# A fused retention, GLU and SwiGLU kernel: the last halved pair sends two sums at once, and the dealer that orders all instructions gets new costs, a second round and 137 shifts

## The chip, the cores and the metric

The kernel runs on one core of one Trainium2 chip. The metric is the device time of one execution in microseconds (us), the median of several runs. Before the change it is 615.1 us (three runs, 614.64 to 616.22).

## The reference, cut to what matters

```python
def reference(q, k, v, moe_w_a, moe_w_b, moe_w_out, moe2_w_gate, moe2_w_val, moe2_w_out, moe2_rms_g):
    # q, k, v: batch 2, 8 heads, 768 positions, head size 64
    for t in range(768):
        state = gamma * state + outer(k[t], v[t])        # per batch and head
        y[t] = q[t] @ state / sqrt(64)
    x = y as 1536 tokens x 512
    x = (x @ w_a) * (x @ w_b) @ w_out                    # feed-forward 0: 512 -> 1536 -> 512
    x = x / sqrt(mean(x * x) + 1e-6) * rms_g             # a norm over the 512 features
    g = x @ w_gate
    return (g * sigmoid(g)) * (x @ w_val) @ w_out        # feed-forward 1
```

## The kernel before, in words

The head of the program (about the first 97 us) computes the retention in chunks of 128 tokens: scores (tiles `sc`), their product with the values (`ya`), the running state (`st`). What follows are the two feed-forward blocks, 0 and 1. Features lie on the partitions, and the 1536 tokens are cut into three blocks j = 0, 1, 2 of 512. Each operand of a large product is split into a high and a low part in fp32r, so that one product of 128 x 128 weights with 512 tokens is three matmuls (high x high, high x low, low x high). In the tables of the trace these are the tiles `c`, `b` and `d` (going up, to 1536 features) and `y` and `x_P` (going down, back to 512).

**Halved products.** The 12 rows of 128 hidden features of a block are taken in pairs; a pair is numbered n = 6 * block + g. The first pair of a block is the opening one, the last the closing one, and the four between are "halved": for the token blocks 0 and 1 the down product is written as seven products of sums, P1 to P7, as in Strassen's scheme. Each exists twice (a and b, for two groups of 128 output features). P1 starts a bank of PSUM, which P6, P5 and P3 then add to (the tile is called `x4_P1_0` for half a of pair 4, whichever product adds to it); P7 starts a second bank, to which P4 adds (`x4_P7_0`); P2 has one to itself (`x4_P2_0`). After most of the products the bank as it then stands is one finished summand of the output. It is read by ScalarE (ACT) into one of four staging slots in SBUF (tiles `z`, in a ring), and sent from there by an accumulating DMA on GpSimd's queue (POOL) to `partial` (block 0) or `out` (block 1) in HBM. P5 has P7's bank added to its slot by VectorE (DVE) first. A halved pair makes 16 such sends, twelve from P products and four from the plain products `J` of token block 2.

```python
CHAIN = ("P1a P1b", "J", "J", "J", "J", "P7a P6a", "P5a P6b", "P4a P3a", "P7b P5b", "P3b P2a", "P4b P2b")
TO = {"P1": (0, 0, None), "P2": (0, 0, None), "P6": (1, 0, None), "P5": (1, 1, "Y2"), "P4": (1, 0, None), "P3": (0, 1, None)}
```

`CHAIN` is the order in which the products are recorded; an entry of `TO` says to which half of the output features and to which token block a sum goes, and which other bank is added. When a halved pair's sends have landed, the closing pair fetches the sums so far back from HBM by `fetch` (six loads of 512 KB into tiles `acc`, on SyncE's queue, SP), adds its own `y` products to them (`collect`, on DVE), and, in block 0, the norm follows: sums of squares over the partitions by matmul (`ms0`, `ms1`, `ms2`, one per token block), a short chain of small instructions on DVE and ACT that ends in `scale`, and a broadcast of it by matmul (`rb0`, `rb1`, `rb2`). `ms` and `rb` share one bank, which four multiplications on DVE read (`acc<-acc,small,rb`). In block 1 the sums are stored to `out`.

**What sets the order.** Nothing is issued as it is written. The kernel records every operation with the ones that it needs (`Plan.record`), an estimate of how long it occupies its engine and when its result is there. `Plan.order` works back from the end and gives each operation a due time. `Plan.list` (the dealer) then deals the operations out one by one: it follows each engine's time by the estimates, and of the operations that are ready takes the one that is due first. The resulting sequence is the program. So a change of an estimate, or a number added to one due time, moves instructions on all engines. Before, the dealer counted 100 ns for any change of the shape of the array's use on TensorE (PE), 100 + 0.83 n ns for any ACT instruction of n elements, and 60 ns from one engine to another.

All instructions of the kernel have one line in the profile, that of the call in `Plan.emit` (L435 before, L474 after); the tiles tell them apart.

Of the kernel before, what the change touches and what calls it, by code (L numbers as in the profile page):

```python
# [38 lines left out]
GRAIN = 4  # L39
AFTER = -1e6  # L40
AHEAD = 25
TURN = 100
TABLE = 1283
SHIFTS = {}
TABLES = AF.Silu, AF.Sqrt
LANES = 8
SOONEST = 12000
# [1 line left out]
DMA = {"load": (2400, 1.0, 600), "store": (700, 1.0, 600), "acc": (1750, 1.0, 600)}  # L49
RATE = {"load": 395, "store": 318, "acc": 145}  # L50
HOP = 120
LEAD = {"vec": 1850, "act": 1750, "gps": 4000}

LINE = 128
# [24 lines left out]
SOON = 400  # L79
GATE = "P5"  # L80
CHAIN = ("P1a P1b", "J", "J", "J", "J", "P7a P6a", "P5a P6b", "P4a P3a", "P7b P5b", "P3b P2a", "P4b P2b")
TO = {"P1": (0, 0, None), "P2": (0, 0, None), "P6": (1, 0, None), "P5": (1, 1, "Y2"), "P4": (1, 0, None), "P3": (0, 1, None)}
FORMS = "opening", *["halved"] * (NG - 2), "closing"
APART = 1
HOLD = {"vec": 1500, "act": 1200, "gps": 4000}
# [131 lines left out]
class Plan:  # L217
# [84 lines left out]
    def order(self):  # L302

        ops = self.ops
        for op in ops:
            for other in op.needs:
                other.next.append(op)
        hop = lambda a, b: (0 if a.engine == b.engine == "pe" and not a.kind else 28 if a.engine == b.engine and not a.kind else 85 if a.kind else 60) + (260 if b.engine == "gps" and b.kind else 0)
        took = lambda op, b: 0 if b.needs[op] == AFTER else DMA[op.kind][0] + DMA[op.kind][1] * op.length + DMA[op.kind][2] + b.needs[op] if op.kind else b.needs[op]
        nominal, t = {}, 0.0  # L310
        for op in ops:
            if op.engine == "pe":
                nominal[op] = t
                t += op.pitch
# [21 lines left out]
        return self.list({op: d + SHIFTS.get(op.name, 0) for op, d in due.items()}, hop)  # L336

    def list(self, due, hop):
        free, shape, table, port = dict.fromkeys(self.engines, 745.0), None, None, {"vec": 0.0, "gps": 0.0}
# [8 lines left out]
        lanes, arriving, queues, clock = {True: [], False: []}, [], {e: [] for e in ("sp", "act", "gps")}, 0.0  # L348

        def finish(op, end):  # L350
            for b in op.next:
# [9 lines left out]
        while len(done) < len(self.ops):  # L361
            best = None
            while at_pe < len(pe) and pe[at_pe] in done:
                at_pe += 1
            for e, some in able.items():
                if e == "pe":
                    last = pe[min(at_pe + AHEAD, len(pe)) - 1].index if at_pe < len(pe) else 0
                    some = [op for op in some if op.index <= last]
                if some:
                    at, lane = free[e], lanes[e == "gps"]  # L370
                    if e in ("sp", "gps") and len(lane) >= LANES and (e == "sp" or all(op.kind for op in some)):
                        if lane[-LANES] not in ended:
                            continue
                        at = max(at, ended[lane[-LANES]] + 85)
                    t = max(at, min(ready[op] for op in some))
                    if best is None or t < best[0]:
                        best = t, e, some
            moving = [q for q in queues.values() if q]
            total = sum(WEIGHT[q[0][1].kind] for q in moving)
            ends = [(clock + q[0][0] * total / WEIGHT[q[0][1].kind], n) for n, q in enumerate(moving)] + [(a[0], -1) for a in arriving]  # L380
            if ends and (best is None or min(ends)[0] <= best[0]):
                now, which = min(ends)
                for q in moving:
                    q[0][0] -= (now - clock) * WEIGHT[q[0][1].kind] / total
# [12 lines left out]
            op = min(now, key=lambda op: (due[op], op.index))  # L397
            if e == "pe":
                t += TURN * (shape not in (None, op.shape))
                shape = op.shape  # L400
            if op.table not in (None, table):
                t += TABLE
                table = op.table
            if op.port:
                t = max(t, port["vec" if e == "gps" else "gps"])
                port[e] = t + op.pitch
            able[e].remove(op)
            done.add(op)
            seq.append(op)
            start[op] = t  # L410
            free[e] = t + op.pitch
            if op.kind:
                arriving.append((t + DMA[op.kind][0], op.index, op))
                lanes[e == "gps"].append(op)
            for b in op.next:
                if b.needs[op] == AFTER:
                    ready[b] = max(ready[b], t)
                elif op.kind:
                    continue
                else:  # L420
                    ready[b] = max(ready[b], t + op.pitch if op.engine == b.engine == "pe" else t + b.needs[op] + hop(op, b))
                free_of(b)
        return max(free.values()), start, seq

# [14 lines left out]
def retention_glu_swiglu(ctx: ExitStack, tc: tile.TileContext, qk, kv, dq, mask, dg, eye, w1, w2, rg, partial, out):  # L439
# [5 lines left out]
    class Engine:  # L445
# [5 lines left out]
        def __getattr__(self, op):  # L451
            def issue(out, *a, **k):
                n = 1
                for size in out.shape[1:]:
                    n *= size
                at = work["pe"] + HOP if after_pe[0] is None else after_pe[0]
                pitch = self.fixed + n * self.each * (0.5 if op == "tensor_scalar" else 1)
# [3 lines left out]
                plan.record(self.name, op, out, a, k, pitch, pitch + 85)  # L461

            return issue

# [633 lines left out]
        collected.add(job)  # L1098
        tick()

    def pour(n, j, m, y, other=None):

        ffn, first = n // NG, FORMS[n % NG] == "opening"
        if (ffn, first) not in stages:
# [6 lines left out]
            act.copy(z, y)  # L1111
        else:
            vec.tensor_copy(z, y)
        if other is not None:
            add(z, z, other)
        to = (out if ffn else partial)[m, j]
        if first:
            dma("sp", to, z, ((ffn, m, j),))
        else:
            dma("gps", to, z, ((ffn, m, j),), accum_op=ALU.add)  # L1120

    def product_of_halves(n, name, i):

# [10 lines left out]
        y = chains[n, tag]  # L1134
# [31 lines left out]
    def do_down(k=1):  # L1166
        for _ in range(k):
# [6 lines left out]
            else:  # L1174
                for name in what.split():
                    product_of_halves(n, name[:2], "ab".index(name[2]))
                    if name == "P3b" and FORMS[g + 1] == "closing":
# [14 lines left out]
    def jobs(ffn, f, j):  # L1192
        n = ffn * NG + f // G
        if f % G == G - 1:
            if FORMS[n % NG] != "halved":
                todo.extend((n, (j, m)) for m in range(KD))
            elif j == 2:
                each = [(2, m) for m in range(KD)]
                todo.extend((n, each.pop(0) if what == "J" else what) for what in CHAIN)


    squaring, turns = [], [*PAIR, 2]
# [371 lines left out]
```

## Time and profile before

| | us |
|---|---|
| median of three runs | 615.1 |
| the profiled execution's own time | 616.86 |
| its span, from the first instruction to the last | 615.1 |
| PE busy | 601.9 |
| DVE busy | 525.4 |
| ACT busy | 418.2 |
| POOL busy | 124.8 |
| sends of 256 KB by accumulating DMA | 128 |

PE is TensorE's matmul unit, DVE VectorE, ACT ScalarE, POOL GpSimd, SP SyncE. Matmuls overlap in the records (one that is listed with 0.39 us starts 0.23 us after the one before), so a PE that is busy all the time is read by the distance of the starts, not by its share.

### The profile page before, as it was taken

How to read it: one execution, taken by the hardware profiler on the slowest of the kernel's cores; microseconds unless marked ns; L12 is line 12 of the kernel's file. 1: busy time of each engine (PE TensorE's matmuls, PEld its weight loads, DVE VectorE, ACT ScalarE, POOL GpSimd, SP SyncE). 2: the span in 40 equal slices, each digit the busy share in tenths (PEclk: the TensorE clock that was granted, in tenths of full speed). 3: DMA queues.
4: the chain of work that ended last, by engine and by line, in shares of the span. 5: the costliest groups of instructions: out<-in, count | busy, mean ns of one | idle time of the engine just before them, and what ended most of it. 6: DMA issues, size and time to landing. Idle time of an engine off the chain costs nothing.

```text
span 615.1 us, 9880 instructions
## 1 busy us (share of the span) xinstructions
PE 601.9 (98%) x3572; PEld 510.8 (83%) x3572; DVE 525.4 (85%) x949; ACT 418.2 (68%) x810; POOL 124.8 (20%) x142
## 2 busy tenths in 40 slices
PE   8999999999999999998999999999999999999997
PEld 8788888888888888886887778888888888888876
DVE  4789997799998997985788999699999899898554
ACT  3674786666886876685456867578888788787530
POOL 1330000013323323333100000001422323323310
PEclk9899999999999999998999999999999999999999
DMA  8984146039988988899950234424997997987895
GB/s 342 387 292 136 45 150 251 24 72 214 184 154 167 166 157 170 152 202 186 219 196 1 69 120 124 168 69 94 194 171 144 185 172 158 169 154 122 121 261 215
DMA packets 41617, 101.15 MB, mean 164 GB/s; under 512 B 4704, under 2 KB 5088, under 8 KB 41568
## 3 DMA queue, kind: packets, MB, share of 16 engines
q0 software_dynamic: 18432, 33.56, 37.8%
q1 hardware_dynamic: 22848, 66.79, 31.8%
q8 instruction: 28, 0.46, 0.3%
q14 instruction: 21, 0.17, 0.1%
q10 hardware_dynamic: 288, 0.17, 0.1%
HBM read 57.51 MB, written 42.99 MB: 163 GB/s over the span
## 4 chain that ended last, share of the span: by engine, by line
PE 86%; DMA 5%; DVE 5%; issue 1%; ACT 1%; DVEq 0%; SPq 0%; POOL 0%; ACTq 0%; POOLq 0%
PE b L435 29%; PE d L435 15%; PE y L435 15%; PE x_P L435 12%; PE c L435 9%; PE ya L435 3%; DVE acc L435 2%; DMA partial<-z 2%; PE sc L435 2%; DMA acc<-out 2%; DMA q<-in_qk 1%; PE w L435 1%; PE st L435 1%; ACT z L435 1%; DVE xl L435 1%
## 5 line engine op out<-in xcount | busy, mean ns | idle before, releaser
L435 POOL DMA_DIRECT2D out<-z x64 | 55.7, 910 | 230.5 <-ACT z L435 198.3
L435 POOL DMA_DIRECT2D partial<-z x64 | 55.9, 914 | 205.0 <-ACT z L435 172.5
L435 ACT COPY z<-x_P 128x512 f32<-128x512 f32 x96 | 55.4, 586 | 34.3 <-PE x_P L435 23.8
L435 PE MATMUL y<-h,o 128*128 128x512 f32 x288 | 68.7, 393 | 2.1 <-DVE acc L435 1.8
L435 PEld LDWEIGHTS y<-h,o 128*128 128x128 f32 x288 | 53.2, 188 | 14.2 <-DVE acc L435 2.7
L435 PE MATMUL b<-xh,uh 128*128 128x512 f32 x160 | 63.0, 394 | 0.0
L435 PE MATMUL b<-xl,uh 128*128 128x512 f32 x160 | 62.8, 392 | 0.0
L435 PE MATMUL b<-xh,ul 128*128 128x512 f32 x160 | 62.3, 389 | 0.0
L435 ACT CAST uh<-wt 128x512 fp32r<-128x512 f32 x82 | 48.9, 621 | 11.6 <-PE d L435 5.8
L435 DVE TENSOR_TENSOR ul<-wt,uh 128x512 fp32r<-128x512 f32 x82 | 53.0, 684 | 1.7 <-ACT uh L435 1.5
L435 PE MATMUL x_P<-r,l 128*128 128x512 f32 x192 | 51.8, 394 | 2.0 <-ACT z L435 2.0
L435 ACT ACTIVATE v<-raw 128x512 int32<-128x512 uint32 x72 | 48.7, 679 | 3.8 <-DMA raw<-in_w 3.4
L435 PE MATMUL y<-h,l 128*128 128x512 f32 x192 | 48.3, 391 | 0.0
L435 PE MATMUL b<-th,uh 128*128 128x512 f32 x120 | 47.7, 398 | 0.0
L435 PE MATMUL b<-tl,uh 128*128 128x512 f32 x120 | 47.6, 396 | 0.0
L435 PE MATMUL b<-th,ul 128*128 128x512 f32 x120 | 47.2, 393 | 0.0
L435 PE MATMUL d<-xh,ul 128*128 128x256 f32 x160 | 45.3, 283 | 0.0
L435 PE MATMUL d<-xl,uh 128*128 128x256 f32 x160 | 45.2, 283 | 0.0
L435 PE MATMUL d<-t,uh 128*128 128x256 f32 x240 | 45.0, 282 | 0.0
L435 PE MATMUL d<-xh,uh 128*128 128x256 f32 x160 | 45.0, 281 | 0.0
L435 PEld LDWEIGHTS d<-t,uh 128*128 128x128 f32 x240 | 40.4, 190 | 3.9
L435 DVE TENSOR_TENSOR g<-g,d 128x256 f32<-128x256 f32 x80 | 33.2, 416 | 11.1 <-PE d L435 5.2
(151 smaller groups left out, 1527.4 us busy)
## 6 DMA issues: line engine op xcount, KB each, us to landing
raw<-in_w SPq DMA_DIRECT2D x72, 512.0 KB, 5.1
partial<-z POOLq DMA_DIRECT2D x64, 256.0 KB, 5.2
out<-z POOLq DMA_DIRECT2D x64, 256.0 KB, 5.2
q<-in_qk SPq DMA_DIRECT2D x12, 512.0 KB, 5.6
k<-in_kv SPq DMA_DIRECT2D x12, 512.0 KB, 6.5
partial<-z SPq DMA_DIRECT2D x12, 256.0 KB, 2.5
acc<-partial SPq DMA_DIRECT2D x6, 512.0 KB, 5.8
out<-z SPq DMA_DIRECT2D x12, 256.0 KB, 2.8
```

The costliest lines, as they stand in the source:

```text
L435: getattr(self.engines[op.engine], method)(real(out), *map(real, args), **{k: real(a) for k, a in kwargs.items()})
```

## The change

The edits are three. First, the last halved pair of each block (pairs 4 and 10) is recorded in another order, and its sends are fewer. P2 is done beside P1 and its bank is added to P1's slot, so that the two go out as one send. P6's bank is copied to a slot that is kept; P4's bank is added to it later by DVE, and the sum goes out as one send. P2's banks are `Y2` and `B0` there. This makes eight fewer ACT copies, eight more DVE additions and eight fewer accumulating DMAs in the program (of 128); the matmuls are the same. The early part of the fetch of token block 1 is still tied to P3b.

Second, the dealer's estimates: the change of geometry on PE costs by kind (110 to 222 ns, 55 more in one case), an ACT instruction has one cost when it reads PSUM and one when it reads SBUF, and the distance between engines is 45 ns without POOL; idle time of PE that adds up is given a price of its own. The due times are computed twice, the second time from the order that the first deal gave. Third, 137 operations have their due time moved by -34 to +60 us.

```diff
-TURN = 100
+TURN = {(64, P): 200, (64, 64): 110, (P, P): 222, (P, 64): 147}
-SHIFTS = {}
+SHIFTS = {
+    4: -17300, 5: -11500, 6: -11100, 7: 3200, 8: -4300, 21: 17250, 36: 6800, 44: -4900, 45: 13450, 87: 21000, 89: 17100, 116: 32500, 117: -23300, 127:
...
+ROUNDS = 2
...
+ACT_COST = {False: (92, 0.836), True: (40, 0.855)}
...
-TO = {"P1": (0, 0, None), "P2": (0, 0, None), "P6": (1, 0, None), "P5": (1, 1, "Y2"), "P4": (1, 0, None), "P3": (0, 1, None)}
+TO = {"P1": (0, 0, None), "P2": (0, 0, None), "P6": (1, 0, None), "P5": (1, 1, "P7"), "P4": (1, 0, None), "P3": (0, 1, None)}
+WHEN = "P3b"
+CHAIN_LAST = ("P2a P1a", "P2b P1b", "J", "J", "J", "J", "P7a P6a", "P5a P6b", "P3a P4a", "P7b P5b", "P3b P4b")
+TO_LAST = {"P1": (0, 0, "P2"), "P6": "keep", "P5": (1, 1, "P7"), "P4": (1, 0, "kept"), "P3": (0, 1, None)}
...
+        pes = [op for op in ops if op.engine == "pe"]
+        for left in reversed(range(ROUNDS)):
+            due = self.dues(pes, took, hop)
+            got = self.list(due if left else {op: d + SHIFTS.get(op.index, 0) for op, d in due.items()}, hop)
+            pes = [op for op in got[2] if op.engine == "pe"]
+        return got
...
             if e == "pe":
-                t += TURN * (shape not in (None, op.shape))
+                if shape not in (None, op.shape):
+                    t += TURN[op.shape] + 55 * (shape == (64, 64) and op.shape == (P, 64))
...
-        tag = "Y2" if name in ("P7", "P4") else f"Y{i}"
+        last = FORMS[n % NG + 1] == "closing"
+        tag = ("Y2", "B0")[i] if last and name == "P2" else "Y2" if name in ("P7", "P4") else f"Y{i}"
...
-        if name in TO:
-            half, j, other = TO[name]
-            pour(n, j, 2 * half + i, y, chains[n, other.format(i)] if other else None)
+        to = (TO_LAST if last else TO).get(name)
+        if to == "keep":
+            chains[n, "kept", i] = stage(n, y)
+        elif to:
+            half, j, other = to
+            if other == "kept":
+                z = chains[n, "kept", i]
+                add(z, z, y)
+                send(n, j, 2 * half + i, z)
+            else:
+                pour(n, j, 2 * half + i, y, chains[n, other, i] if other else None)
```

Three places show how the dealt order moved. In all rows the number at the end of a name counts operations and differs between the two programs.

The first is ACT in the second half of pair 4, the last halved pair of block 0. Rows `z1_0` and `z1_1` fill the staging slots; `s9`, `t9`, `u9` free the bank `b1_9` of the up product beside it. Before:

```order
L435 COPY z1_0_1586<-x4_P1_1_2988 128x512
L435 COPY s9_3108<-b1_9_3090 128x512
L435 CAST h0_10_0_3114<-s8_2946 128x512
L435 COPY z1_0_1586<-x4_P7_0_3057 128x512
L435 CAST o10_3121<-wl10_3040 128x512
L435 COPY z1_1_1654<-x4_P1_0_2954 128x512
L435 COPY z1_1_1654<-x4_P1_1_2988 128x512
L435 COPY t9_3142<-b1_9_3090 128x512
L435 ACTIVATE wt12_3155<-raw12_0_3102 128x2x256
L435 COPY z1_0_1586<-x4_P1_1_2988 128x512
```

After the change, at the same place:

```order
L474 COPY s9_3101<-b1_9_3079 128x512
L474 CAST h0_10_1_3116<-u8_3077 128x512
L474 ACTIVATE v12_0_3124<-raw12_0_3088 128x512
L474 COPY z1_0_1534<-x4_P1_0_2901 128x512
L474 CAST o10_3139<-wl10_3055 128x512
L474 CAST h0_10_0_3142<-s8_2951 128x512
L474 COPY t9_3153<-b1_9_3079 128x512
L474 ACTIVATE wt12_3157<-raw12_0_3088 128x2x256
L474 COPY z1_1_1663<-x4_P1_1_2969 128x512
L474 COPY u9_3174<-b1_9_3079 128x512
L474 COPY z1_1_1663<-x4_P1_1_2969 128x512
```

Before, the copy of `x4_P7_0` (P4a) stands ahead of those of P3a and P5b. It is gone after the change: P4a's bank is read by DVE, which adds it to a slot that was filled at P6a. On PE, P7b, the next user of that bank, stood behind six matmuls after P4a before (P5b and P3a), and now stands behind 33: P3a, P5b and P3b of pair 4 and four blocks of six matmuls `b` lie between.

The second place is SP at the end of the program: the six loads of the sums so far for the closing pair of block 1, and the first store. The first number in `acc1_1_0` is the block, the second the token block j, the third the half of the output features. Before:

```order
L435 DMA acc1_1_1_6061<-out_0 128x2x512
L435 DMA acc1_2_1_6075<-out_0 128x2x512
L435 DMA acc1_2_0_6090<-out_0 128x2x512
L435 DMA acc1_1_0_6092<-out_0 128x2x512
L435 DMA acc1_0_0_6154<-out_0 128x2x512
L435 DMA acc1_0_1_6179<-out_0 128x2x512
L435 DMA out_0<-acc1_1_0_6092 128x512 x2
```

After:

```order
L474 DMA acc1_2_1_5962<-out_0 128x2x512
L474 DMA acc1_2_0_6080<-out_0 128x2x512
L474 DMA acc1_1_1_6083<-out_0 128x2x512
L474 DMA acc1_1_0_6108<-out_0 128x2x512
L474 DMA acc1_0_0_6137<-out_0 128x2x512
L474 DMA acc1_0_1_6148<-out_0 128x2x512
L474 DMA out_0<-acc1_1_0_6108 128x512 x2
```

The two loads of token block 2 moved to the front, ahead of the two of token block 1. On PE, the blocks between P3b of pair 10, whose send `acc1_1_0` waits for, and the first closing product `y68` were 33 matmuls of 512 columns and 36 of 256, and are 27 and 30 now; three closing products of six matmuls follow before `y71`, which needs the bank of `y68` again.

The third place is DVE in the norm, from the reciprocal of token block 2 to its `scale`. `o12` and `o13` are the out weights that `y40` and the products after it read. Before:

```order
L435 RECIPROCAL small_84<-small_84 128x4
L435 ISA u12_2_3593<-u12_2_3593,v12_2_3596 128x1024
L435 TENSOR_TENSOR small_84<-small_84 128x4
L435 ISA u13_2_3598<-u13_2_3598,v13_2_3608 128x1024
L435 SCALAR_TENSOR_TENSOR small_84<-small_84 128x4
L435 TENSOR_TENSOR g17_3633<-g17_3633,c17_1_3624 128x512
L435 SCALAR_TENSOR_TENSOR small_84<-small_84 128x4
L435 TENSOR_TENSOR acc0_1_1_3251<-acc0_1_1_3251,acc0_0_0_3365 128x1024
L435 CAST scale_3479<-small_84 128x4
L435 TENSOR_TENSOR g18_3685<-g18_3685,c18_1_3678 128x512
L435 TENSOR_TENSOR scale_3479<-small_84,scale_3479 128x4
```

After:

```order
L474 RECIPROCAL small_84<-small_84 128x4
L474 TENSOR_TENSOR o12_3624<-u12_2_3529,o12_3624 128x512
L474 TENSOR_TENSOR small_84<-small_84 128x4
L474 TENSOR_TENSOR h1_1_1_3644<-g16_3604,h1_1_1_3644 128x512
L474 SCALAR_TENSOR_TENSOR small_84<-small_84 128x4
L474 TENSOR_TENSOR o13_3646<-u13_2_3546,o13_3646 128x512
L474 SCALAR_TENSOR_TENSOR small_84<-small_84 128x4
L474 TENSOR_TENSOR acc0_1_0_3239<-acc0_1_1_3259,acc0_1_0_3239 128x1024
L474 CAST scale_3423<-small_84 128x4
L474 TENSOR_TENSOR g17_3668<-g17_3668,c17_1_3626 128x512
L474 TENSOR_TENSOR scale_3423<-small_84,scale_3423 128x4
```

The out weights' `o12` and `o13` now stand inside the chain, ahead of `scale`; before, they stood behind it. On PE, 36 matmuls of 512 columns lie between `ms2` and `rb2` now, and 30 before.

## Rows read from the trace of the kernel before

**Rows 1.** Page, part 1: busy us, share of the span, instructions.

```profile
PE 601.9 (98%) x3572; PEld 510.8 (83%) x3572; DVE 525.4 (85%) x949; ACT 418.2 (68%) x810; POOL 124.8 (20%) x142
```

**Rows 2.** Stages: us, busy us (instructions) per engine, PE clock, DMA share, GB/s.

```profile
100.00:283.00 183.00, 183.00 (x962) 157.34 (x961) 165.01 (x305) 128.00 (x244) 49.52 (x57) 1.00 0.80 159
...
306.00:358.00 52.00, 48.73 (x257) 40.15 (x256) 47.33 (x91) 35.10 (x55) 0.00 (x0) 1.00 0.27 87
358.00:597.00 239.00, 239.00 (x1246) 204.64 (x1245) 208.25 (x377) 177.47 (x342) 55.70 (x64) 1.00 0.74 153
...
286.40:289.80 3.40, 3.40 (x10) 2.63 (x9) 1.30 (x2) 1.06 (x3) 2.25 (x3) 0.50 0.80 100
```

**Rows 3.** Timeline of PE near 286 us: start, us, instruction, idle before.

```profile
285.83 1.18 PE L435 MATMUL x_P<-r,l 128*128 128x512 f32 x3 [1.97 <-ACT z L435]
286.80 0.63 PE L435 MATMUL b<-th,uh 128*128 128x512 f32 x1
287.23 0.63 PE L435 MATMUL b<-tl,uh 128*128 128x512 f32 x1
...
290.27 0.40 PE L435 MATMUL b<-xh,uh 128*128 128x512 f32 x1
290.50 0.40 PE L435 MATMUL b<-xl,uh 128*128 128x512 f32 x1
```

**Rows 4.** Chain of waits, 278 to 299 us: start, us, what.

```profile
278.52 6.57 DMA partial<-z
...
285.19 0.59 ACT z L435
...
285.83 1.18 PE x_P L435 x3
...
297.27 1.43 PE d L435 x12
```

**Rows 5.** Groups by line: busy us, mean ns, idle before.

```profile
L435 ACT COPY z<-x_P 128x512 f32<-128x512 f32 x96 | 55.4, 586 | 34.3 <-PE x_P L435 23.8 <-issue 5.6 <-DMA partial<-z 1.9
...
L435 DVE TENSOR_TENSOR z<-z,x_P 128x512 f32<-128x512 f32 x16 | 10.9, 681 | 1.6 <-ACT z L435 1.6
```

**Rows 6.** Page, part 6: DMA issues, KB each, median us to landing.

```profile
partial<-z POOLq DMA_DIRECT2D x64, 256.0 KB, 5.2
```

**Rows 7.** Timeline of PE in the closing of block 0 and the norm.

```profile
312.98 1.66 PE L435 MATMUL y<-h,o 128*128 128x512 f32 x6 [0.42 <-DVE acc L435]
...
329.99 1.02 PE L435 MATMUL ms<-small,sq 128*128 128x1 f32 x8 [0.74 <-DVE acc L435]
...
341.74 0.95 PE L435 MATMUL ms<-small,sq 128*128 128x1 f32 x8
...
350.90 0.30 PE L435 MATMUL rb<-ident,scale 128*128 128x128 f32 x1 [1.24 <-DVE scale L435]
351.47 1.00 PE L435 MATMUL rb<-ident,scale 128*128 128x128 f32 x7 [0.27 <-DVE scale L435]
...
353.93 3.24 PE L435 MATMUL y<-h,o 128*128 128x512 f32 x13 [0.26 <-DVE o L435]
```

**Rows 8.** Chain of waits, 575 us to the end.

```profile
580.90 1.36 PE x_P L435 x6
...
586.95 11.12 DMA acc<-out
```

**Rows 9.** Timeline of PE at the end.

```profile
598.90 12.58 PE L435 MATMUL y<-h,o 128*128 128x512 f32 x54 [1.34 <-DVE acc L435]
```

**Rows 10.** Timeline of DVE at the end.

```profile
611.52 0.76 DVE L435 TENSOR_TENSOR acc<-y,acc 128x256 f32<-128x256 f32 x2 [0.67 <-PE y L435]
```

**Rows 11.** DMA issues from 560 us on.

```profile
out<-acc SPq DMA_DIRECT2D x11, 256.0 KB, 2.1
```

**Rows 12.** Timeline of PE in the head.

```profile
24.96 0.50 PE L435 MATMUL c<-xh,uh 128*128 128x512 f32 x1
25.30 0.40 PE L435 MATMUL c<-xh,ul 128*128 128x512 f32 x1
```

More of the change, by code (lines that the diff above doesn't have):

```diff
@@ L41 @@
 AHEAD = 25
-TURN = 100
+TURN = {(64, P): 200, (64, 64): 110, (P, P): 222, (P, 64): 147}
 TABLE = 1283
-SHIFTS = {}
+SHIFTS = {
[12 rows of a table added]
+}
+ROUNDS = 2
+SLOW = 3414
+MOST = 2000
 TABLES = AF.Silu, AF.Sqrt
@@ L307, in order, with dues @@
                 other.next.append(op)
-        hop = lambda a, b: (0 if a.engine == b.engine == "pe" and not a.kind else 28 if a.engine == b.engine and not a.kind else 85 if a.kind else 60) + (260 if b.engine == "gps" and b.kind else 0)
+        hop = lambda a, b: (0 if a.engine == b.engine == "pe" and not a.kind else 28 if a.engine == b.engine and not a.kind else 85 if a.kind else 60 if "gps" in (a.engine, b.engine) else 45) + (235 if b.engine == "gps" and b.kind else 0)
         took = lambda op, b: 0 if b.needs[op] == AFTER else DMA[op.kind][0] + DMA[op.kind][1] * op.length + DMA[op.kind][2] + b.needs[op] if op.kind else b.needs[op]
+        pes = [op for op in ops if op.engine == "pe"]
[4 more added lines that the diff above has]
+        return got
+    def dues(self, pes, took, hop):
+        ops = self.ops
         nominal, t = {}, 0.0
[L311 to L314, printed above, removed]
+        for op in pes:
+            nominal[op] = t
+            t += op.pitch
         due, back = {}, {}
@@ L335, in order @@
                     heapq.heappush(heap, (-limit[a], -a.index))
-        return self.list({op: d + SHIFTS.get(op.name, 0) for op, d in due.items()}, hop)
+        return due
     def list(self, due, hop):
@@ L347, in list @@
         at_pe, done, start, ended, seq = 0, set(), {}, {}, []
-        lanes, arriving, queues, clock = {True: [], False: []}, [], {e: [] for e in ("sp", "act", "gps")}, 0.0
+        lanes, arriving, queues, clock, gaps, slow = {True: [], False: []}, [], {e: [] for e in ("sp", "act", "gps")}, 0.0, [], 0.0
         def finish(op, end):
@@ L406, in list @@
                 port[e] = t + op.pitch
+            pitch = op.pitch
+            if e == "pe" and t > 8000:
+                if t > free[e] + 1:
+                    gaps.append((free[e], t))
+                    while gaps[0][1] < t - SLOW:
+                        gaps.pop(0)
+                    if t >= slow and sum(b - max(a, t - SLOW) for a, b in gaps) > MOST:
+                        slow = t + SLOW
+                if t < slow:
+                    pitch = min(2 * pitch, pitch + slow - t)
             able[e].remove(op)
@@ L410, in list @@
             start[op] = t
-            free[e] = t + op.pitch
+            free[e] = t + pitch
             if op.kind:
@@ L420, in list @@
                 else:
-                    ready[b] = max(ready[b], t + op.pitch if op.engine == b.engine == "pe" else t + b.needs[op] + hop(op, b))
+                    ready[b] = max(ready[b], t + pitch if op.engine == b.engine == "pe" else t + b.needs[op] + pitch - op.pitch + hop(op, b))
                 free_of(b)
@@ L456, in issue @@
                 at = work["pe"] + HOP if after_pe[0] is None else after_pe[0]
-                pitch = self.fixed + n * self.each * (0.5 if op == "tensor_scalar" else 1)
+                ins = [v for v in (*a, *k.values()) if isinstance(v, View)]
+                banks = any(v.tile.pool.kinds for v in ins)
+                fixed, each = ACT_COST[banks] if self is act else (self.fixed, self.each)
+                pitch = fixed + n * each * (0.5 if op == "tensor_scalar" else 1)
+                pitch += 95 * (self is act and isinstance(k.get("scale"), View)) + 50 * (op == "scalar_tensor_tensor" and isinstance(a[1], View))
+                pitch += 45 * (self is act and any(v.dims[-1][0] > 1 for v in ins))
                 work[self.name] = max(work[self.name], at) + pitch
@@ L460, in issue @@
                 ends[0] = max(ends[0], last[0])
-                plan.record(self.name, op, out, a, k, pitch, pitch + 85)
+                plan.record(self.name, op, out, a, k, pitch, pitch + (105 if self is act else 85))
             return issue
@@ L1099, in down, with stage @@
         tick()
-    def pour(n, j, m, y, other=None):
+    def stage(n, y):
         ffn, first = n // NG, FORMS[n % NG] == "opening"
@@ L1113, in pour, with send @@
             vec.tensor_copy(z, y)
-        if other is not None:
-            add(z, z, other)
+        return z
+    def send(n, j, m, z):
+        ffn = n // NG
         to = (out if ffn else partial)[m, j]
-        if first:
+        if FORMS[n % NG] == "opening":
             dma("sp", to, z, ((ffn, m, j),))
@@ L1120, in pour @@
             dma("gps", to, z, ((ffn, m, j),), accum_op=ALU.add)
+    def pour(n, j, m, y, other=None):
+        z = stage(n, y)
+        if other is not None:
+            add(z, z, other)
+        send(n, j, m, z)
     def product_of_halves(n, name, i):
@@ L1176, in do_down @@
                     product_of_halves(n, name[:2], "ab".index(name[2]))
-                    if name == "P3b" and FORMS[g + 1] == "closing":
+                    if name == WHEN and FORMS[g + 1] == "closing":
                         after(FETCH, lambda: fetch(ffn, 1))
@@ L1198, in jobs @@
                 each = [(2, m) for m in range(KD)]
-                todo.extend((n, each.pop(0) if what == "J" else what) for what in CHAIN)
+                todo.extend((n, each.pop(0) if what == "J" else what) for what in (CHAIN_LAST if FORMS[n % NG + 1] == "closing" else CHAIN))
     squaring, turns = [], [*PAIR, 2]
```

2 lines of the change are left out of this document (1 added, 1 removed), and 11 rows, old and new, of the table SHIFTS.

## The prediction

> **What bounds the kernel now.** I read first how the span divides over the engines: PE is busy for 98% of it [rows 1]. Then the stages. From 100 to 283 us and from 358 to 597 us PE shows no idle time at all at the full clock [rows 2], and there the change, which leaves the matmuls as they are, has nothing to win. What it can win lies between these stages. The waits of PE over 0.2 us that I find behind the head stand in three places, and I went to each with the timeline and the chain of waits.
>
> The first is at 285.83 us: a product of pair 4 waits 1.97 us for an ACT copy into a staging slot [rows 3]. The chain shows why: that copy, 0.59 us long, waited for a send that took 6.57 us to land, because the slot that it fills was still being sent [rows 4]. So this stage is bound by the round of four slots, not by PE. Just behind the wait PE's clock falls to 0.50 of full speed, its lower level of 1.2 GHz, for 3.4 us [rows 2]: the matmuls of `b` start 0.43 us apart there and 0.23 us apart at 290.27 [rows 3]. For counting I use 0.227 us for a matmul of 512 columns and 0.119 us for one of 256, from runs of 6 and of 12 of them [rows 4, 8].
>
> The second place is the closing of block 0 and the norm. From 306 to 358 us PE is busy for 48.73 of 52.00 us [rows 2]; the larger waits are 0.42 us (a bank of `y` that DVE has yet to read), 0.74 us (`ms0`, behind the multiplications by `rb1`), 1.24 and 0.27 us (`rb2`, for the two parts of `scale`) and 0.26 us (the out weights) [rows 7]. The third is the end: `y71` waits 1.34 us [rows 9], because the load of the sums so far, issued at 586.95 us, took 11.12 us [rows 8].
>
> **The change part by part.** The sum is made on the profiled execution's span, 615.1 us, which is also the median of the runs; the 616.86 us of that execution itself are 1.8 us of surroundings that an unprofiled run doesn't show.
>
> *Pair 4's slots.* The product that waited is P7b, for P4a's bank. After the change no copy into a new slot frees that bank: DVE adds it to a slot that P6a filled long before. Between P4a and P7b there are 33 matmuls now, 33 x 0.227 = 7.5 us, and an addition like that takes 0.68 us [rows 5]. So the wait goes (-2.0) and with it, as I expect, the fall of the clock (3.4 x 0.5 = -1.7): -3.7. At worst both stay (0); more than -3.7 isn't there to win.
>
> The wait that could take its place: P5b's copy goes into the slot of P4a's sum, so it must wait for that send to land, and P3b on PE waits for the copy. From the end of P4a to P3b, PE has 30 matmuls, 30 x 0.227 = 6.8 us. The other side needs an addition (0.68), the landing (5.2 us in the median) and the copy (0.59) [rows 5, 6]: 6.5 us if nothing is queued ahead, 7.8 us with 6.57 us of landing as in the chain [rows 4]. That is a wait of 0 to 1.0 us; I take +0.4. A wait of 2.0 us with 1.7 of clock behind it would be the state before again. In pair 10 the same path has 9.0 us of cover (30 matmuls of 512 columns, 18 of 256), so nothing. The Trainium skill, in DMA: Bandwidth & Descriptors (section Anatomy of one DMA), gives a DMA from GpSimd as about 2.0 us and its bytes by 436 GB/s, which would be an estimated 2.6 us for these 256 KB. Half the median of the rows, so I go by the rows; by the page this term would be 0 and the time 0.4 us less.
>
> *The eight additions and copies.* 8 x 0.68 = 5.4 us more on DVE, 8 x 0.59 = 4.7 us less on ACT [rows 5]. They lie beside PE's work in stages where DVE is busy for 165.01 of 183 and 208.25 of 239 us [rows 2]; 2.7 us per block fit. If DVE had no room there, they would cost 2.7 us in each block. I cost them at nothing.
>
> *The norm.* `rb2` had 30 matmuls behind `ms2`, and its second part came 351.47 - 341.74 = 9.73 us after `ms2`, the first 9.16 us [rows 7]. Now there are 36, that is 6 x 0.227 = 1.4 us more, against 9.16 and 9.73 us that DVE's chain needs if it stays as long: it has the same small instructions, with seven large ones in between where there were eight. Of the 1.51 us some 0.5 stays: -1.0. The bank of `y` gets seven blocks instead of four until it is written again, and `o12` and `o13` now stand ahead of `scale`: -0.4 and -0.3. `ms0` has to wait for four multiplications that read the bank of `rb1`, with 2.8 us of `d` blocks as cover where there were 4.1 us of `y`; DVE has less between them. I leave its wait as it is. Together -1.7. From below, all 3.3 us go. From above, `ms0` and the product `c17_0` behind it lose 2 us: +2.0.
>
> *The end.* The loads of token block 2 are ahead of the two that matter, and four fewer sends are on their way beside them (two of them stood behind P3b). P3b ended at 580.90 + 0.68 = 581.58, the load was issued 5.4 us later [rows 8]. From P3b to `y71` there are 45 matmuls of 512 columns and 30 of 256 now, 45 x 0.227 + 30 x 0.119 = 13.8 us; before it was 51 and 36, 15.9 us, and the wait. So the load may take 13.8 - 5.4 = 8.4 us. With half of what it shared the DMA engines with gone, I estimate 6 to 7 of its 11.12 us: -1.3 for the wait (bounds 0 and -1.3). The last product is now one whose addition isn't cut in two: 0.68 us and then a store of 256 KB, 2.1 us in the median [rows 5, 11]. Before, both halves were added after 0.76 us [rows 10] and half the store was in flight by then: +0.2, bounds 0 and +0.7 (a third of that store).
>
> *Geometry.* The order of the program has 56 changes of geometry instead of 60, the four fewer all in the head. The first `c` after the state's matmuls is followed by the next after 0.34 us instead of 0.23 [rows 12], 0.11 us for a change: -0.4, between 0 and twice that. Up to the fourth chunk PE's order and the set of loads ahead of it are the same, so the start isn't faster.
>
> *Closer reuse of banks.* The new order is denser: a bank is written again behind only one block of other work in 41 places, where there were 15 (a `b` bank after 1.4 us 16 times against 9, a `d` bank after 0.7 us 6 times against 2, the rest among `x_P`, `b3` and `d3`). The 15 of before cost nothing, and a copy of 0.59 us [rows 5] fits into 1.4 us. But when another ACT instruction of 0.6 us is ahead of it in a place of 0.7 us, it doesn't. Between 0 and 26 x 0.6 = 15.6 us; the rows stand at nothing, I take +0.5.
>
> Sum: -3.7 + 0.4 - 1.7 - 1.3 + 0.2 - 0.4 + 0.5 = -6.0, so **609.1 us**.
>
> **The rivals.** (1) *The slots bind again.* The four slots are still a round, and a kept slot is held longer, from P6 to the landing of P4. If P5b's copy comes 2 us late, the clock falls as it did, and of the first term only the waits that moved are left: +3.3 on the forecast, 612.4 us. For it: sends were the bound of that stage. Against: the pair has 12 sends instead of 16. Chance 0.14. (2) *The norm empties.* All its waits go, the closer reuse costs nothing and the kept slot neither: -1.6 - 0.5 - 0.4, 606.6 us. For it: each of these waits is on a chain of small instructions that a few moved rows relieve. Chance 0.22. (3) *Slower: the closer reuse.* In the 26 added places PE waits for the reader of the bank, all over the two stages that had no wait. ACT is busy for 177.47 of 239 us there [rows 2], so an instruction is often ahead. From 0.3 us per place the sum turns: 26 x 0.3 = 7.8 us take the gain and more, 616.4 us, and 0.4 us give 619.0. Against: 15 such places show nothing. Chance 0.07 for over 616.9 us, 0.05 for between. (4) *The change of the sends works, the new deal does nothing*: the norm, the geometry and the banks stay as they are, and -3.7 + 0.4 - 1.3 + 0.2 = -4.4 is left, 610.7 us. For it: the estimates that changed differ by some tens of ns per instruction, and PE has no wait in most of the program. Against: the norm's rows did move. Chance 0.08.
>
> **How the numbers follow.** The forecast has a chance of 0.44, with 607.5 to 610.6 us for its own range; rival 2 has 0.22, rival 1 0.14, rival 4 0.08, rival 3 0.07 and 0.05. A difference of 0.3% (1.8 us) is about what a measurement can tell here. Slower is rival 3's 0.07; the same is its 0.05 and the upper edge of rival 1 (0.03); faster is the rest, 0.85. The range goes from 605.2 (rival 2 with the geometry at its bound, 606.2, and 1 us for stages that I counted as they are) to 613.3 us (rival 1 with the closer reuse at 1.4 instead of 0.5).
>
> **What would show it.** Right: no fall of the clock near 286 us, no wait of P7b; a load of `acc` near 580 us that lands in under 8.4 us and `y` products without a break to the end; a wait of about 0.5 us at `rb2`; 60 accumulating sends per block in place of 64. Wrong: PE idle behind P5b in pair 4 with ACT waiting for a landing; many waits of 0.2 to 0.6 us of PE for ACT between 100 and 283 or 358 and 597 us; a new wait at `c17_0`.

## The result and the profile after

The changed kernel takes 609.36 us in the median of six runs (606.94 to 611.52), the kernel before beside it 615.09; the ratio is 0.9905, 95% interval 0.9877 to 0.9932. That is 5.7 us less, where 6.0 were forecast. The places are not those of the forecast.

First the engines of the changed kernel (busy us, share, instructions), as in [rows 1]:

```profile
PE 598.6 (98%) x3572; PEld 509.6 (84%) x3572; DVE 528.8 (87%) x957; ACT 413.6 (68%) x802; POOL 117.1 (19%) x134
```

The eight additions and copies are there (957 for 949 on DVE, 802 for 810 on ACT, 8 fewer instructions on POOL). Next the stages, as in [rows 2]: us, busy us (instructions) of PE, PEld, DVE, ACT and POOL, PE's clock, DMA share, GB/s.

```profile
240.00:292.00 52.00, 49.04 (x232) 40.18 (x231) 40.40 (x71) 33.50 (x63) 15.91 (x20) 1.00 0.89 166
306.00:358.00 52.00, 50.95 (x257) 42.43 (x256) 50.20 (x94) 35.64 (x56) 0.00 (x0) 0.97 0.23 81
358.00:597.00 239.00, 239.00 (x1248) 205.27 (x1247) 208.56 (x382) 171.75 (x336) 52.15 (x60) 1.00 0.71 153
...
323.25:326.66 3.41, 3.41 (x9) 2.66 (x9) 3.23 (x8) 1.99 (x4) 0.00 (x0) 0.50 0.00 0
```

Two things are to be seen: PE is idle for 3 us around the last halved pair (240 to 292 us), and there is one stretch of the slower clock, now at 323 us, in the norm. Before, one lay at 286 us [rows 2] and another in the head, which is shown below. The waits themselves, in the timeline of PE (start, us, instruction, idle before):

```profile
250.55 0.96 PE L474 MATMUL x_P<-h,l 128*128 128x512 f32 x3 [1.14 <-ACT z L474]
...
273.81 0.97 PE L474 MATMUL x_P<-r,l 128*128 128x512 f32 x3 [1.68 <-ACT z L474]
...
321.68 1.02 PE L474 MATMUL ms<-small,sq 128*128 128x1 f32 x8 [0.76 <-DVE acc L474]
...
346.83 1.00 PE L474 MATMUL rb<-ident,scale 128*128 128x128 f32 x8
...
588.59 16.51 PE L474 MATMUL y<-h,o 128*128 128x512 f32 x72
```

The waits at `rb2` and at the end [rows 7, 9] are gone, and the 72 closing matmuls run without a break. P7b of pair 4 doesn't wait any more [rows 3]. In its place two other products wait for a copy into a slot: P3b of pair 3 (250.55) and P5a of pair 4 (273.81). They wait for the copies of P5b of pair 3 and of P6a of pair 4. The timeline of ACT says what those two copies waited for; the last line has the times from issue to landing of the sends of `z` between 238 and 276 us:

```profile
249.91 0.58 ACT L474 COPY z<-x_P 128x512 f32<-128x512 f32 x1 [1.02 <-DMA partial<-z]
...
273.17 0.58 ACT L474 COPY z<-x_P 128x512 f32<-128x512 f32 x1 [2.15 <-DMA partial<-z]
...
DMA to landing us min/median/max: 3.8/5.2/8.2
```

The two sends that these copies waited for were issued at 242.4 and 266.5 us and took 7.4 and 6.5 us to land. So the slots still bind. The head has changed as well. The first line is of the kernel before, the second of the changed kernel at the same scores (`sc`; its 30 matmuls are the 16 of the first line and the 14 ahead of them):

```profile
16.87 2.08 PE L435 MATMUL sc<-q 64*128 64x128 f32 x16 [1.13 <-DMA q<-in_qk]
```

```profile
14.44 2.14 PE L474 MATMUL sc<-q 64*128 64x128 f32 x30 [0.80 <-ACT xf L474]
```

Before, `sc` waited 1.13 us for a load of `q`, and a stretch of the slower clock began at the end of that wait (mean clock 0.79 from 13 to 21 us); afterwards neither is there, in this execution.

To set all this against the terms I use one table, worked out from the traces. All kernels here have the same 3572 matmuls. From the start of each matmul I take off the usual distances of the starts of all matmuls ahead of it (0.2265 us for 512 columns, 0.119 for 256, 0.05 to 0.11 for the small ones); what the remainder grows by within a stage is the time that PE lost there, through waits, a slower clock or changes of geometry. The head is given against the kernel before, since its distances are the least sure. One profiled execution each, us:

| kernel | head | 97-240 | 240-292 | 292-358 | 358 to last matmul | behind it | span |
|---|---|---|---|---|---|---|---|
| before | 0 | 1.2 | 4.2 | 6.2 | 4.2 | 4.0 | 615.1 |
| before, second profile | -0.1 | 1.2 | 2.5 | 6.9 | 3.0 | 4.0 | 612.7 |
| changed | -3.2 | 1.6 | 4.2 | 5.0 | 1.9 | 4.2 | 608.9 |
| changed, second profile | -2.9 | 1.3 | 3.1 | 3.9 | 1.8 | 4.2 | 606.7 |
| sends_alone | +1.3 | 1.3 | 1.1 | 9.2 | 2.9 | 4.0 | 615.0 |
| dealer_alone | +0.3 | 2.4 | 2.9 | 7.9 | 2.6 | 4.0 | 615.2 |
| no_shifts | +0.3 | 3.4 | 5.8 | 5.9 | 3.1 | 3.9 | 617.6 |
| shifts_head | -2.7 | 2.6 | 2.8 | 10.5 | 2.8 | 4.0 | 615.2 |
| shifts_late | +1.7 | 3.6 | 5.7 | 10.9 | 3.3 | 4.2 | 624.7 |
| loads_unshifted | 0.0 | 2.0 | 3.5 | 8.1 | 3.9 | 4.2 | 616.8 |
| half_sends | -3.1 | 1.3 | 0.6 | 2.7 | 1.9 | 4.2 | 602.8 |
| half_loads | -1.2 | 1.3 | 0.8 | 3.9 | 1.8 | 4.2 | 606.1 |
| p5a_later | -3.2 | 1.3 | 2.7 | 2.9 | 2.1 | 4.2 | 605.3 |
| two_later | -3.1 | 1.3 | 3.5 | 5.0 | 1.9 | 4.2 | 608.0 |

### The profile page after: what moved, and what is told of

Same layout as the page of the kernel before. It is cut to its first block, busy times and chain, and to the rows that moved or that the text cites. A ratio compares the mean times of both kernels' runs of the same rounds, so it can differ in the third digit from the quotient of the medians.

```text
span 608.9 us, 9865 instructions
## 1 busy us (share of the span) xinstructions
PE 598.6 (98%) x3572; PEld 509.6 (84%) x3572; DVE 528.8 (87%) x957; ACT 413.6 (68%) x802; POOL 117.1 (19%) x134
## 5 line engine op out<-in xcount | busy, mean ns | idle before, releaser
L474 POOL DMA_DIRECT2D out<-z x60 | 52.2, 896 | 234.3 <-ACT z L474 188.7
L474 POOL DMA_DIRECT2D partial<-z x60 | 52.4, 881 | 205.7 <-ACT z L474 161.8
L474 ACT COPY z<-x_P 128x512 f32<-128x512 f32 x88 | 51.2, 589 | 25.1 <-PE x_P L474 15.0
L474 DVE TENSOR_TENSOR g<-g,d 128x256 f32<-128x256 f32 x80 | 33.1, 415 | 10.9 <-ACT g L474 6.5
```

Of the source, the lines that this page charges most:

```text
L474: getattr(self.engines[op.engine], method)(real(out), *map(real, args), **{k: real(a) for k, a in kwargs.items()})
```

## The experiments

My theory after the result was that of the forecast with other places: the fewer sends relieve the slots, and the new deal empties the head, the norm and the end. The rivals were that the sends do nothing by themselves, and that the 137 shifts, not the new costs, do the work.

**sends_alone**, the first edit on the kernel before:

```diff
+CHAIN_LAST = ("P2a P1a", "P2b P1b", "J", ...)
+TO_LAST = {"P1": (0, 0, "P2"), "P6": "keep", ...}
 (with stage, send and product_of_halves as in the change; old dealer)
```

> The kernel before with the new sends of the last halved pair alone: old dealer, one round, no shifts. By the prediction's theory (the fewer sends free the slots of pair 4, -3.7 +0.4, and relieve the loads at the end, up to -1.3) about 611 us, and no wait of PE over 1 us for a copy into a slot between 240 and 290 us. By the rival (the gain comes from the new deal; a slot wait only moves to another product of pairs 3 and 4) 614 to 616 us with a slot wait of 1 to 2 us somewhere between 240 and 290 us.

Measured: 615.82 us, ratio 1.002 (0.9995 to 1.0046). Both theories are half right: the slot wait is gone, as the forecast had it, and the time is that of the rival. The stage of the slots is all but free of waits, and the norm gives it back: the first row is the stage, the second a stretch of the slower clock that begins just behind `rb2`, in the norm (columns as above), then the timeline of PE.

```profile
240.00:292.00 52.00, 51.68 (x249) 43.04 (x249) 45.09 (x81) 35.94 (x68) 15.63 (x18) 1.00 0.83 158
...
350.59:357.42 6.83, 5.80 (x15) 4.18 (x14) 6.82 (x10) 6.41 (x10) 0.00 (x0) 0.50 0.00 0
```

```profile
349.05 0.30 PE L438 MATMUL rb<-ident,scale 128*128 128x128 f32 x1 [1.78 <-DVE scale L438]
349.62 1.00 PE L438 MATMUL rb<-ident,scale 128*128 128x128 f32 x7 [0.27 <-DVE scale L438]
350.45 0.60 PE L438 MATMUL y<-h,o 128*128 128x512 f32 x1
352.08 1.22 PE L438 MATMUL y<-h,o 128*128 128x512 f32 x2 [1.03 <-DVE h L438]
```

The lost time in the slots' stage falls to 1.1 us (4.2 and 2.5 in the two profiles of the kernel before), and in the norm it rises to 9.2 (from 6.2 and 6.9). Of the 9.2 us, 3.4 are the slower clock: 6.83 us at half speed. That is not this execution alone: the mean granted clock of the 12 runs is 0.993, that of the 34 of the kernel before beside them 0.996, a difference of some 1.8 us. The slot edit works where it is; the order that the old dealer makes of it loses as much elsewhere. (The 1.3 us of the head are not of the order, which is the same there on PE: the slower clock lasted 6.83 us where it lasted 3.41 before.)

**dealer_alone** and **no_shifts**, the new costs and both rounds without shifts, with the old and the new sends:

```diff
-SHIFTS = {4: -17300, ...}
+SHIFTS = {}
 (dealer_alone also: CHAIN and TO for every halved pair)
```

> The new dealer (costs, two rounds) with the old sends and no shifts. By the prediction's theory the slots of pair 4 bind as before: 613 to 615 us, with the wait of about 2 us near 286 us. By the rival (the deal gives the gain) 610 to 612 us, with the 3 us of the head and the norm's wait at rb2 gone.

> The changed kernel without its 137 shifts: new sends, new costs, two rounds. If the shifts are small trim, 609 to 611 us, as the changed kernel. If the shifts are what empties the head, the norm and the end, 613 to 616 us, and the waits of PE in these three places are back or stand elsewhere.

Measured: dealer_alone 619.42 us, ratio 1.0058 (1.0033 to 1.0083); no_shifts 617.58 us, 1.0052 (1.0031 to 1.0073). The new costs with the second round make the kernel slower by about 0.5%, some 3.3 us, with either kind of sends. Both are slower than any of the theories had it. In dealer_alone the wait near 286 us that I expected isn't there. The slot wait, 2.35 us, is at P5a of pair 4, for P6a's copy, and in the norm `ms0` waits 3.41 us for DVE. The waits of PE in no_shifts, 97 us to the end (us in total, times, longest), and the copy of the longest one in ACT's timeline:

```profile
PE x_P L461 <- ACT z L461: 3.5, 1, 3.5
PE d L461 <- DVE g L461: 0.9, 1, 0.9
```

```profile
278.98 0.58 ACT L461 COPY z<-x_P 128x512 f32<-128x512 f32 x1 [3.18 <-DMA partial<-z]
```

Here too it is P5a that waits, for P6a's copy. With the new sends and without shifts that wait is nearly twice as long as the 1.97 us that the edit was to remove, and the slower clock follows it. So the wait at P6a's copy comes with the new dealer's order: it stands with the old sends as with the new. By the two ratios (1.0052 and 0.9905) the shifts are worth 1.5%, some 9 us, on top of these costs and sends.

**shifts_head**, **shifts_late** and **loads_unshifted** take the shifts apart:

```diff
+SHIFTS = {k: v for k, v in SHIFTS.items() if k < 300}    # shifts_head
+SHIFTS = {k: v for k, v in SHIFTS.items() if k >= 300}   # shifts_late
+SHIFTS = {k: v for k, v in SHIFTS.items() if k not in (4, 5, 6, 7, 8)}   # loads_unshifted
```

> The changed kernel with the 30 shifts of operations of the head alone (those recorded before number 300). Without any shift it took 617.6 us, with all 609.4. If the head's shifts carry what the traces show there (3.4 us between the kernel without shifts and the changed one), 613 to 615 us, with no late load near 15 us and no slower clock behind it. If the gain needs all of them at once, 616 to 618 us.

> The changed kernel with the 107 other shifts alone. If the parts add up, 611 to 613 us: the head as without shifts (an excess 3.4 us larger than in the changed kernel), the rest as in the changed kernel, with slot waits of about 3 us together between 240 and 280 us. If the order behind the head hangs on how the head ended, the waits stand elsewhere and the time is 614 us or more.

> The changed kernel without the shifts of its first five loads (operations 4 to 8), which put the first raw weights ahead of k and the mask. If the head's 3.2 us came from the order of these loads, the late q load near 15 us is back and the excess of the head at 97 us is 3 us larger; then 612 us or more, since the order behind it moves too. If the head's gain is in the order of PE and DVE in the chunks behind it, the head stays within 1 us of the changed kernel's.

The table has 26 shifts of the head and 111 others, not 30 and 107. Measured: 616.71 us (1.0038, 1.0011 to 1.0065), 622.48 us (1.0119, 1.0085 to 1.0153) and 617.88 us (1.0055, 1.0029 to 1.008). The shifts of the head do take the head's 2.7 us away, but the norm behind it loses 10.5 us, 3.4 of them at the slower clock. The others without those of the head are the slowest kernel of all. That they fit only the order that stands behind the new head is my reading of these three times; it isn't shown otherwise. Without the shifts of five loads the head is as before (0.0), and the late `q` is back:

```profile
17.27 1.16 PE L475 MATMUL sc<-q 64*128 64x128 f32 x16 [1.50 <-DMA q<-in_qk]
```

So the shifts don't add up: each part alone leaves a kernel slower than the one before, all of them together one that is 5.7 us faster. No run has the shifts with the old sends or the old costs, so what they owe to either is not separated.

**before_again** and **after_again** are the two kernels unchanged, for a second profile.

> The kernel before, unchanged, for a second profile: what of its waits is the same in another execution. By the prediction the wait near 286 us with the slower clock behind it belongs to the order and stands again (1.5 to 2.2 us); the 1.13 us in the head behind a late load with the slower clock behind it may be chance. Time 614 to 616 us, ratio 1.000 within 0.002.

> The changed kernel, unchanged, for a second profile and more times: 608 to 611 us. If its two slot waits of 1.14 and 1.68 us at 249 and 272 us belong to its order, both stand again within 0.5 us; if they were chance of one execution, one of them is gone.

Measured: 614.49 us (0.9999, 0.9981 to 1.0017) and 608.27 us (0.9911, 0.988 to 0.9941). In the second profile of the kernel before, a copy waits for a landing again, but it is another one: P4a's copy was in time there and P7b had 0.14 us of idle time ahead of it. The copy of P5b, two copies later, is late, and P3b waits for it (timeline of PE, then of ACT):

```profile
287.68 0.96 PE L435 MATMUL x_P<-h,l 128*128 128x512 f32 x3 [1.57 <-ACT z L435]
```

```profile
287.04 0.58 ACT L435 COPY z<-x_P 128x512 f32<-128x512 f32 x1 [2.32 <-DMA partial<-z]
```

No slower clock followed it there (that stretch lies at 351 us in this profile, behind `rb2`). So a slot wait of 1.6 to 2 us stands in both profiles, and neither the product that waits nor the fall of the clock behind it is the same. In the changed kernel the same two slot waits stand again, shorter: 0.87 and 0.56 us, the second by more than the 0.5 us that I had allowed (the lost time in the stage is 3.1 for 4.2 us).

**half_sends** and **half_loads** ask what makes the slots late. The order is that of the changed kernel, on every engine for the first, on PE and POOL for the second.

```diff
+            some = slice(0, TB // 2 if n in (3, 4) else TB)
+            dma("gps", to[:, some], z[:, some], ...)     # half_sends
+            some = slice(0, DM if half else 2 * DM)      # six loads of raw weights
+            dma("sp", t...[:, some], src[:, some], ...)  # half_loads
```

> The changed kernel in the same order, but the accumulating sends of pairs 3 and 4 carry half of their sums' tokens (the other half is left out of the output). If the two waits of the changed kernel at 249 and 272 us (1.14 and 1.68 us) hang on how long the sends take to land, the landings fall from 5 us in the median and up to 8 to about 3, both waits go, and the time is 606 to 607 us. If the waits come from ACT's order or from something else that the sends only accompany, they stay and the time is 609 to 610 us.

> The changed kernel with the six weight loads of 512 KB that run beside pairs 3 and 4 cut to half their bytes (the rest of these weights is left as an earlier load left it); PE and POOL have the same order, three ACT instructions and one of DVE stand a place later. If the sends land late because these loads share the DMA engines with them, landings of over 6 us between 236 and 276 us (eight in the changed kernel) become rare, the slot waits shrink, and the time is 605 to 607 us, as with sends of half the bytes. If the sends are late by their own number alone, landings and waits stay and the time is 608 to 609 us.

Measured: 604.87 us (0.9834, 0.9804 to 0.9864) and 606.73 us (0.9881, 0.9859 to 0.9902). In both, PE has next to no idle time left between 240 and 292 us; the first row is of half_sends, the second of half_loads, and the last two are the landings of `z` from 236 to 292 us in the same order:

```profile
240.00:292.00 52.00, 52.00 (x251) 43.47 (x250) 44.06 (x77) 37.07 (x68) 17.50 (x21) 1.00 0.68 124
```

```profile
240.00:292.00 52.00, 51.96 (x248) 43.06 (x247) 43.60 (x77) 37.07 (x69) 18.47 (x22) 1.00 0.92 148
```

```profile
DMA to landing us min/median/max: 2.9/3.4/6.4
```

```profile
DMA to landing us min/median/max: 4.0/5.0/7.6
```

In the changed kernel the same landings are 3.8, 5.1 and 8.2 us (least, median, most). It is the landing of the sends that holds the slots: with half their bytes and nothing else changed the waits are gone. The stage's lost time of 3.1 and 4.2 us falls to 0.6, so 2.5 to 3.6 us is what the slots still cost the changed kernel. (That half_sends is under the 606 to 607 us that I expected goes with the norm: it loses 2.7 us there for 5.0 and 3.9, with no stretch of the slower clock.) With half the loads the waits are gone too, but landings over 6 us did not become rare, as I had expected of that theory: four sends had them between 236 and 276 us, where six and five have them in the two profiles of the changed kernel. (The eight that I gave ahead of that run don't come out of the trace: it is six sends and five loads.) All six of the changed kernel's had one or two loads of 512 KB under way beside them, and other sends too. Three ACT instructions stand a place later in half_loads as well, so the share of the loads isn't separated from the sends' own number or from that.

**p5a_later** and **two_later** try to cover the two waits with other matmuls:

```diff
+SHIFTS[1230] = 2500                        # p5a_later: P5a of pair 4
+SHIFTS.update({1230: 2500, 1101: -850})    # two_later: P3b of pair 3 too
```

> The changed kernel with one more shift: P5a of pair 4 (operation 1230) is due 2.5 us later, and the six matmuls of the plain product y27 go ahead of it; nothing else on PE moves. If the wait of 1.68 us there is only a wait for the slot of P6a, the six matmuls (6 x 0.227 = 1.4 us) cover most of it and the time is 1.0 to 1.5 us under that of the changed kernel run beside it. If the wait moves on to the next product that needs a slot, the time is the same within 0.3 us.

> The changed kernel with P5a of pair 4 later, as in the run ahead, and P3b of pair 3 (operation 1101) 3 us later too, so that a block b and two blocks d go ahead of it. If both waits are covered, 2 to 3 us under the changed kernel, and up to 1.5 us more if the slower clock at 323 us goes with them: 605 to 608 us. If P3b's later send makes a later copy wait for its slot, the gain of the second shift is lost again and the time is that of the run ahead.

Measured: 608.05 us (0.9895, 0.9872 to 0.9919) and 608.37 us (0.99, 0.9875 to 0.9924), the same as the changed kernel beside them (608.27). In p5a_later the wait moved on, from P5a to P4a (PE, then DVE):

```profile
280.71 0.97 PE L475 MATMUL x_P<-r,l 128*128 128x512 f32 x3 [1.16 <-DVE z L475]
```

```profile
279.97 0.68 DVE L475 TENSOR_TENSOR z<-z,x_P 128x512 f32<-128x512 f32 x1
```

P4a adds to P7a's bank, so it waits until DVE has added that bank to P5a's slot, and P5a now comes later. In two_later the wait at P3b of pair 3 is gone, but P5a waits 1.50 us all the same and P4a 1.17. The stage loses 2.7 and 3.5 us, within what the changed kernel loses (3.1 and 4.2): these two moves only decide which product waits. Other orders can do better, as the 1.1 us of sends_alone with the same sends shows.

## Why the prediction was right in the sum and wrong in its places

The means of two profiles each, 613.9 and 607.8 us, are set against the terms. First the ground of the sum. The 1.8 us between 616.86 and 615.1 us are not something that an unprofiled run doesn't show: every run has them (606.94 us with a span of 605.2, for one that wasn't profiled). So the execution that I read was 1.8 us slower than the median, and that its span equals the median of the runs is chance.

- *Pair 4's slots, -3.7 + 0.4.* The stage lost 3.4 us before and loses 3.7 now, so nothing is gained. The step that failed is "so the wait goes": I followed P7b's bank, which is free, and P5b's slot, and went no further back. P5b's copy does wait for its landing, 1.04 us, and leaves P3b 0.14 and 0.42 us of idle time in the two profiles, about the 0.4 that I had. What I left out are the copies ahead of it. I had P6a fill its kept slot "long before" and gave that copy no wait; it waits 2.15 us, and P5b's of pair 3 waits 1.02. The landings behind them (6.5 and 7.4 us) are near the 6.57 of [rows 4], so it is the copies that I missed more than the price of a landing. And of the 3.7 us, the 1.7 of the clock were there in one of the two profiles of before only. That the edit can free this stage is shown by sends_alone (1.1 us). It is rival 1's mechanism, in two places that I hadn't named, and at about its price (3.3 us on the forecast, 3.6 measured), though no slower clock followed. The price that I gave by the Trainium skill, an estimated 2.6 us for such a send (DMA: Bandwidth & Descriptors, section Anatomy of one DMA), is under every landing of 256 KB in this stretch (3.8 us at the least), and the trace decides.
- *The head, -0.4 for its geometry and else nothing.* It measured -3.0, the largest single gain. The step that failed is "so the start isn't faster": the set of loads ahead of the `q` that was late is the same, but their order isn't. That load of `q` landed at 16.8 us in all three profiles with the head of before, and between 15.4 and 16.8 in the seven with the new order of loads; `sc` waited for it in all three, and in two of the seven (0.6 and 1.0 us). Why it can land earlier no run shows. About 1.2 us of the gain remain even when it is late (half_loads, where `sc` waits 1.03 us for `q` and the slower clock comes with it); the rest, 1.7 to 2.0 us, is the late load and the clock. The count of geometry changes was wrong as well: by the shapes of the weights in the two traces there are 42 before and 35 now, seven fewer and not four. At 0.11 us each that is an estimated 0.8 of the 1.2 us.
- *The norm, -1.7.* The stage from 292 to 358 us measured -2.1 (6.6 to 4.5). `rb2`, the bank of `y` and the out weights don't wait at all now, a better outcome than the 0.5 that I had left at `rb2`; `ms0` still waits 0.76 us as assumed, and a stretch of the slower clock follows it, 3.41 us at half speed, which I had not counted.
- *The end, -1.3 + 0.2.* It measured -1.7 from 358 us to the last matmul, though the wait at `y71` was 0.51 and not 1.34 us in the second profile of before, and +0.2 behind. The load that was to take 6 to 7 us took 6.6 and 6.0.
- *Closer reuse, +0.5.* +0.3 between 97 and 240 us and nothing between 358 us and the end. Rival 3 did not occur.
- *Rival 4* (the sends work and the deal does nothing) is refuted, and so is the idea beneath the forecast that each edit brings its own part: the sends alone bring nothing in the total, the new costs lose some 3.3 us, and the table of shifts on top of both turns this into a gain.

The sum was right because a miss of 3.6 us at the slots and one of 2.6 us in the head have opposite signs, with the smaller misses making up the rest. That is luck: the time lay in the range for reasons that the forecast had only in part.

## What to carry to other kernels

In a kernel whose order comes from a planner, an edit is worth what the new order makes of it: time the edit alone, the costs alone and the hand-fitted numbers alone before crediting any of them. A wait for a slot in a ring of transfers need not go with the instruction that waited: here it moved to two other copies. Follow the ring back through every copy that fills a slot, and price the landings with what runs beside them at that place, not with the median of the program. Numbers made for one order (due times by operation) can be worth nothing, or less, on another: parts of this table gave 1.0038 and 1.0119.

## What the runs showed of the hardware that was not expected

The same wait in the same order does not always bring the slower clock. `ms0` waits 0.8 us for DVE in six traces with the same matmuls around it: in four the clock falls behind it (both profiles of the changed kernel, half_loads and two_later), in two it doesn't (half_sends and p5a_later). In half_loads the slots' stage ahead of it has next to no idle time, so the waits there don't decide it either. The rows are of p5a_later and of the second profile of the changed kernel, around that wait:

```profile
318.00:324.00 6.00, 5.22 (x28) 4.10 (x28) 6.00 (x13) 4.00 (x8) 0.00 (x0) 1.00 0.01 3
```

```profile
318.50:324.85 6.35, 5.57 (x22) 4.23 (x21) 5.80 (x12) 4.06 (x7) 0.00 (x0) 0.73 0.01 3
```

In the first the clock stays at its full 2.4 GHz, in the second it is at 1.2 GHz for 3.41 us of the stretch. What decides between them no run here shows. The fall of the clock is one source of the spread of single runs: of the 12 of the changed kernel, five with a mean granted clock of 0.999 or more took 606.9 to 609.0 us, three with 0.994 took 610.8 to 611.8. A price put on a fall of the clock is that of a chance.

The quickest send of half the bytes lands 0.9 us sooner than the quickest whole one (2.9 us in half_sends, 3.8 in the changed kernel). By these two, some 2 us of the 3.8 don't go with the bytes, which is an estimate. In the changed kernel a send of 256 KB took 4.0 to 5.1 us where no load was under way (issued from 251 to 260 us), and up to 8.2 us beside two loads of 512 KB and three other sends (266 to 271 us).
